# Choosing experts behind the mask and the state's sum: three edits to the VectorE order of a gated recurrence with a cosine router

## The chip, the cores and the metric

The kernel runs on one core of one Trainium2 chip. A core has five engines that run side by side, each through its own queue in order: TensorE (PE in the profile), VectorE (DVE), ScalarE (ACT), GpSimd (POOL) and SyncE (SP), which only starts transfers. The metric is the device time of one execution in microseconds, lower is better; for the kernel before it is the median of five runs.

## The reference

```python
def _attn_ref(q, k, v, alpha):            # (4, 8, 768, 48) each, float32
    state = np.zeros((B, H, D, D))
    for t in range(S):
        state = alpha[:, :, t, :, None] * state + np.einsum('bhd,bhe->bhde', k[:, :, t], v[:, :, t])
        y[:, :, t] = np.einsum('bhd,bhde->bhe', q[:, :, t], state)

def _moe_ref(x, expert_emb, tau, w1, w2): # x: y as (3072, 384) rows; E = 8, F = 1024
    logits = normalized(x) @ normalized(expert_emb).T / tau
    expert_idx = np.argmax(logits, axis=1)
    gate_w = softmax(logits)[np.arange(N), expert_idx]
    for e in range(E):
        mask = expert_idx == e
        h = np.maximum(x[mask] @ w1[e], 0.0)
        out[mask] = gate_w[mask, None] * (h @ w2[e])
```

A gated linear recurrence gives 3072 tokens of 384 numbers; each token goes to the one of eight experts with the largest cosine logit, and the expert's two-layer network, scaled by the softmax weight, is its output.

## The kernel before

The work has two stages. The first does the recurrence in 24 chunks of 128 tokens (NS = 24; six chunks per batch, NCH = 6) and routes the tokens as they come. The second runs the eight experts, one after the other, on the rows sorted by expert. Only the first stage and the turn to the second are touched.

The first stage is a software pipeline. In step s, TensorE in this order turns the alpha, key and query tiles of chunk s (results pa, pk, pq), makes the token rows and logits of chunk s-3 (`rows`, results pyx and px), the scores of chunk s-1 (sc), the output columns of chunk s-2 (`mix_states`, `mix_chunk`), the state's update of chunk s-1 (pd), and turns the decayed keys back (pkb; that belongs to chunk s and is issued at the head of step s+1). The steps can be told apart by the first matmul of pa: 4.70 us is step 0, 81.42 is step 14, 86.33 step 15, 121.88 step 21.

VectorE's regular share of a step is: the scan r (L477), the decayed keys kr (L484), a reciprocal ini (L502), the scan a (L506), the sum of the logits x (L653), the causal mask of one half of the scores, sm (L577), and the state's sum (L558 or L560). A chunk that is the last of its batch has no state update, so no state's sum in the step after. GpSimd multiplies the queries with a (qs, L510), masks the other half of the scores (affine_select, L579), and decays the state (dec, L535; end, L515). ScalarE copies results out of PSUM. The transposes share three PSUM buffers in turn; pd and px share one buffer (tag "mm"), so px of a step can be written only when the state's sum of the step before has read pd.

Routing works on eight groups of chunks:

```python
GROUPS = ((0, 4), (4, 8), (8, 12), (12, 14), (14, 16), (16, 20), (20, 23), (23, 24))
```

Once the rows of a group's last chunk are there, `choose` picks the experts of the group: top (L330), win (L332), win times first (L333), best (L335), chosen (L337), all on VectorE, and then one running sum per chunk, `before` (L340), on GpSimd or, for chunks 15 and 23, on VectorE. This happens at the end of steps 6, 10, 14, 16, 18, 22 and in the two steps after the loop's last chunk. Two or four steps later `place` turns the sums into row numbers with TensorE, and the tokens are scattered to DRAM (`to_rows`, indirect transfers issued by GpSimd), one or two per step.

After chunk 15 is placed, `first_expert` finds which expert is run first (L375 to L389, on VectorE). SyncE needs its result `turn_i` for `fetch_early` (L181), which also waits for the scatters of the first 16 chunks, and for the weights of the first expert (L141). `counts` (L395 to L425) prepares the rest after the last group.

Engines execute in the order in which the program issues, except that a scheduler may move an instruction ahead of others that do not depend on it. `tc.issue_after(x)` keeps what is issued under it behind instruction x on x's own engine; it is an order, not a wait between engines. `behind(s)` is that for the scan a and for qs of step s. Before the change nothing held the choice back, and in the built program it stood between x and sm.

Of the kernel before, what the change touches and what calls it, by code (L numbers as in the profile page):

```python
# [12 lines left out]
ALU = mybir.AluOpType  # L13
# [14 lines left out]
def kernel(  # L28
# [12 lines left out]
    nc = tc.nc  # L41
# [3 lines left out]
    P = 128  # L45
    DP = 64
    NP = H // 2
    NCH = S // P
    N = B * S
    NS = N // P  # L50
# [15 lines left out]
    S0, EARLY = 16, 2  # L66
# [12 lines left out]
    causal = consts.tile([P, 1, P], FP32)  # L79
# [120 lines left out]
    with ExitStack() as c1:  # L200
# [122 lines left out]
        def choose(g):  # L323

            s0, s1 = GROUPS[g]
            n = s1 - s0
            shp = [P, n, E]
            l = x_g[g][:, :, LG : LG + E]
            top = work.tile([P, GMAX], FP32, name="top")[:, 0:n]
            nc.vector.tensor_reduce(top.unsqueeze(2), l, axis=AX.X, op=ALU.max)  # L330
            win = work.tile([P, GMAX, E], FP32, name="win")[:, 0:n]
            nc.vector.tensor_tensor(win, l, bc(top, shp, 2), ALU.is_equal)  # L332
            nc.vector.tensor_tensor(win, win, bc(first, shp, 1), ALU.mult)  # L333
            best = work.tile([P, GMAX], FP32, name="best")[:, 0:n]
            nc.vector.tensor_reduce(best.unsqueeze(2), win, axis=AX.X, op=ALU.max)  # L335
            ch = chosen[:, s0:s1]
            nc.vector.tensor_tensor(ch, win, bc(best, shp, 2), ALU.is_equal)  # L337
            for s in range(s0, s1):
                eng = nc.vector if s in (S0 - 1, NS - 1) else nc.gpsimd
                eng.tensor_tensor(before[:, s + 1], before[:, s], chosen[:, s], ALU.add)  # L340

        def place(g, total=False):
# [29 lines left out]
        def first_expert(n):  # L372

            ok = work.tile([P, E], FP32, name="ok")
            nc.vector.scalar_tensor_tensor(  # L375
                out=ok, in0=n, scalar=float(EARLY * P), in1=first, op0=ALU.is_ge, op1=ALU.mult
            )
            lead = work.tile([P, 1], FP32, name="lead")
            nc.vector.tensor_reduce(lead, ok, axis=AX.X, op=ALU.max)
            nc.vector.tensor_scalar(lead, lead, -1.0, float(E), ALU.mult, ALU.add)  # L380
            nc.vector.tensor_scalar(turn_f, cols, lead, None, ALU.add)
            wrap = work.tile([P, E], FP32, name="wrap")
            nc.vector.tensor_scalar(wrap, turn_f, float(E), float(E), ALU.is_ge, ALU.mult)
            nc.vector.tensor_tensor(turn_f, turn_f, wrap, ALU.subtract)
            nc.vector.tensor_copy(turn_i, turn_f[0:1])
            r0 = work.tile([1, E], FP32, name="r0")
            nc.vector.tensor_scalar(r0, turn_f[0:1], float(N), None, ALU.mult)
            nc.vector.tensor_scalar(r0[:, 0:1], r0[:, 0:1], float(EARLY * P), None, ALU.add)
            nc.vector.tensor_copy(row0, r0)  # L389

        def counts(n):

            shp = [P, E, E]
            mine = work.tile(shp, FP32, name="mine", bufs=1)
            nc.vector.tensor_tensor(  # L395
                mine, bc(turn_f, shp, 2), bc(cols, shp, 1), ALU.is_equal
            )
            nc.vector.tensor_tensor(mine, mine, bc(n, shp, 1), ALU.mult)
            r = work.tile([P, E], FP32, name="rows_of", bufs=1)
            nc.vector.tensor_reduce(r.unsqueeze(2), mine, axis=AX.X, op=ALU.add)  # L400

            row = work.tile([P, E], FP32, name="pad_row", bufs=1)
            nc.vector.tensor_scalar(row, r, part, None, ALU.add)
            end_i = work.tile([P, E], I32, name="end_i", bufs=1)
            nc.vector.tensor_scalar(end_i, r, float(P - 1), None, ALU.add)
            nc.vector.tensor_scalar(end_i, end_i, -P, None, ALU.bitwise_and)
            end = work.tile([P, E], FP32, name="end_f", bufs=1)
            nc.vector.tensor_copy(end, end_i)
            nc.vector.tensor_tensor(end, row, end, ALU.is_ge)
            nc.vector.tensor_scalar(end, end, float(FAR), None, ALU.mult)  # L410
            nc.vector.tensor_tensor(row, row, end, ALU.add)
            nc.vector.scalar_tensor_tensor(
                out=pads, in0=turn_f, scalar=float(N), in1=row, op0=ALU.mult, op1=ALU.add
            )
            nc.vector.tensor_scalar(
                extra, r[0:1], float(HALF - 1 - NC * P), 0.0, ALU.add, ALU.max
            )
            nc.vector.tensor_scalar(extra, extra, 6, None, ALU.arith_shift_right)
            nc.vector.tensor_reduce(most, extra, axis=AX.X, op=ALU.max)
            nc.vector.tensor_scalar(  # L420
                r[:, 0:1], r[:, 0:1], float(-EARLY * P), None, ALU.add
            )
            shp = [P, E, NC + 1]
            nc.vector.tensor_tensor(used, bc(r, shp, 2), bc(starts, shp, 1), ALU.is_gt)
            return nc.vector.tensor_copy(used_i, used[0:1])  # L425
# [31 lines left out]
        def behind(s):  # L457

            queue = ExitStack()
            for call in st[s]["last"]:  # L460
                queue.enter_context(tc.issue_after(call.ins))
            return queue
# [76 lines left out]
        def update(s):  # L539

            c = s % NCH
            if c == NCH - 1:
                return
            d = st[s]
            kb, vt = d["kb"], vt_s[s % NBV]
            pd = ps_mm.tile([P, NP, DP], FP32, tag="mm", name="pd")
            for p in range(NP):
                for hh in range(2):
                    h = 2 * p + hh
                    mm(  # L550
                        pd[DP * hh : DP * hh + DP, p],
                        lhsT=kb[:, h * DP : (h + 1) * DP],
                        rhs=vt[:, h],
                        start=True, stop=True,
                    )
            carried["state"] = state = work.tile([P, NP, DP], FP32, name="state")
            if c == 0:
                nc.vector.tensor_copy(state, pd)  # L558
            else:
                nc.vector.tensor_tensor(state, pd, d["dec"], ALU.add)  # L560

        def scores(s):

            d = st[s]
            kr, qs = d["kr"], d["qs"]
            d["sm"] = sm = [work.tile([P, NP, P], FP32, name=f"sm{hh}") for hh in range(2)]
            sc = [ps_sc.tile([P, NP, P], FP32, name=f"sc{hh}") for hh in range(2)]
            for p in range(NP):
                for i in range(2):
                    to = slice(i * HALF, (i + 1) * HALF)  # L570
                    for hh in range(2):
                        sl = slice(DP * hh, DP * hh + DP)
                        mm(
                            sc[hh][to, p], lhsT=kr[sl, p, to], rhs=qs[sl, p],
                            start=True, stop=True, skip_group_check=True,
                        )
            nc.vector.tensor_tensor(sm[0], sc[0], causal.to_broadcast([P, NP, P]), ALU.mult)  # L577
            nc.scalar.copy(sm[1], sc[1])
            d["masked"] = nc.gpsimd.affine_select(  # L579
                out=sm[1], in_=sm[1], pattern=[[0, NP], [1, P]], base=0,  # L580
                channel_multiplier=-1, compare_op=ALU.is_ge, fill=0.0,
            )
# [115 lines left out]
        def placing(s):  # L698

            n = None  # L700
            for g in placed_at.get(s, ()):
                r = GROUPS[g][1] - 1
                with in_turn():
                    n = place(g, r in (S0 - 1, NS - 1))
                if r == S0 - 1:
                    lead.append(n)
            return n

        lead = []
# [6 lines left out]
        for s in range(NS + 3):  # L716
# [72 lines left out]
            if s >= NS:  # L789
                n = placing(s)  # L790
            if lead:
                with behind(s):
                    first_expert(lead.pop())
            with behind(s) if s < NS else tc.issue_after(st[NS - 1]["masked"].ins):
                n_now = len(send) if s >= NS else 0 if s == NS - 1 else 1 + (len(send) > 2)
                for c in send[:n_now]:
# [8 lines left out]
            for r in rows_of(s):  # L805
                g = group_of[r]
                if r == GROUPS[g][1] - 1:
                    choose(g)
                    with behind(s) if s < NS else ExitStack():
                        nc.gpsimd.tensor_copy(x_g[g][:, :, TK], toks[:, slice(*GROUPS[g])])  # L810
            if s > NS:
                with in_turn():
                    first_layer_early(2 * (s - NS) + 2, 2 * (s - NS) + 4)
        routed = [counts(n)]
        for i in range(2):
            routed.append(to_rows(pads[:, i : i + 1], blank))
            fetch(i)
# [2 lines left out]
    with ExitStack() as c3:  # L820
# [155 lines left out]
        dve = []  # L976
# [408 lines left out]
```

## Time and profile before

| what | value |
|---|---|
| median of 5 runs | 417.6 us (415.79 to 418.26) |
| the profiled execution | 415.63 us, span 413.8 us |
| granted TensorE clock, mean | 0.993 |
| VectorE, GpSimd, ScalarE busy | 69%, 54%, 47% of the span |
| first stage, turn, experts | about 5 to 150, 150 to 168, 168 to 408 us |
| TensorE busy in these | 137.2 of 145, 16.8 of 18, 238.3 of 240 us |

The span runs from the first to the last instruction. The profile counts an engine as busy while it executes; TensorE's matmuls overlap, so its busy share is an upper look at its use. In a timeline line stand the start, the duration, engine, line and operation, what is written and read, and in brackets the idle time before it with what ended it.

### The profile page before, as it was taken

What the parts mean: (1) busy time and instruction counts of PE and PEld (TensorE: products, weight loads), DVE (VectorE), ACT (ScalarE), POOL (GpSimd) and SP (SyncE); (2) the same over time, 40 slices, a digit from 0 to 9 for tenths busy, and PEclk for the clock granted to TensorE, in tenths of its full rate; (3) what the DMA queues carried; (4) which work ended last, traced back from release to release, by engine and by line L of the source; (5) the groups of instructions that cost most, each with busy time, mean ns of one, the idle gap of its engine ahead of it and who ended that gap; (6) DMA issues with size and microseconds to landing.
All of it is one profiled execution on the core that took longest, in us unless ns stands there. A gap on an engine that the chain in (4) does not pass through costs nothing. (4 is left out here: it accounts for less than half of the span.)

```text
span 413.8 us, 12552 instructions
## 1 busy us (share of the span) xinstructions
PE 396.0 (96%) x4954; PEld 353.2 (85%) x4954; DVE 287.2 (69%) x634; ACT 195.4 (47%) x481; POOL 221.7 (54%) x288
## 2 busy tenths in 40 slices
PE   6999999999999999999999999999999999999994
PEld 6889889888888767679989989899979979979974
DVE  7898979699799616862696695791594389397530
ACT  4455544555445524463653734823651572662320
POOL 7455587767765546721853934822761581582001
PEclk9999999999999999999999999999999999999998
DMA  9999999987996993695505606505601900101001
GB/s 139 157 165 157 148 205 180 189 181 164 202 175 131 331 344 134 168 367 197 203 16 171 246 18 224 183 19 184 226 19 41 359 9 19 41 0 41 17 16 44
DMA packets 119379, 60.28 MB, mean 146 GB/s; under 512 B 102287, under 2 KB 113816, under 8 KB 119312
## 3 DMA queue, kind: packets, MB, share of 16 engines
q1 hardware_dynamic: 115208, 49.14, 50.0%
q0 software_dynamic: 3728, 10.16, 6.8%
q8 instruction: 46, 0.75, 0.8%
q14 instruction: 21, 0.17, 0.1%
q10 hardware_dynamic: 376, 0.05, 0.1%
HBM read 49.69 MB, written 11.45 MB: 148 GB/s over the span
## 5 line engine op out<-in xcount | busy, mean ns | idle before, releaser
L852 POOL DMA_INDIRECT out_dram<-y,sx x25 | 24.6, 985 | 102.8 <-DVE y L1161 42.3
L982 DVE TENSOR_TENSOR hT<-pq,hT 128x512 f32<-128x512 f32 x63 | 43.6, 692 | 46.2 <-PE pq L1082 44.3
L1082 PE MATMUL pq<-xT_m,w_m 128*128 128x128 f32 x560 | 67.2, 275 | 0.0
L1082 PEld LDWEIGHTS pq<-xT_m,w_m 128*128 128x128 f32 x560 | 64.7, 192 | 0.3 <-issue 0.3
L510 POOL TENSOR_TENSOR qs<-qc,a 128x512 f32<-128x512 f32 x24 | 30.7, 1277 | 36.7 <-DVE a L506 19.7
L1034 POOL TENSOR_TENSOR w_m<-w_m,w 128x512 f32<-128x512 f32 x30 | 43.2, 1449 | 1.4
L965 PE MATMUL pyo<-w,hT 128*128 128x384 f32 x128 | 42.6, 486 | 0.0
L1082 PE MATMUL pq<-xT_m,w 128*128 128x128 f32 x280 | 38.4, 277 | 0.6
L987 ACT ACTIVATE hT<-hT 128x512 f32<-128x512 f32 x35 | 22.1, 631 | 31.3 <-DVE hT L982 31.3
L1082 PEld LDWEIGHTS pq<-xT_m,w 128*128 128x128 f32 x280 | 34.9, 192 | 2.1 <-issue 1.8
L965 PEld LDWEIGHTS pyo<-w,hT 128*128 128x128 f32 x128 | 23.7, 190 | 14.8
L477 DVE TENSOR_TENSOR_SCAN r<-pa,inr 128x511 f32<-128x511 f32 x24 | 29.2, 1216 | 6.5 <-PE pa L194 4.7
L191 PE MATMUL sc<-qs,kr 64*64 64x128 f32 x768 | 29.5, 272 | 2.6 <-issue 2.6
L311 POOL DMA_INDIRECT xs<-x,dest x24 | 24.2, 1010 | 11.6 <-DVE x L653 6.7
L506 DVE TENSOR_TENSOR_SCAN a<-pa,ini 128x512 f32<-128x512 f32 x24 | 29.3, 1222 | 1.0
L1154 PE MATMUL pq<-w_m,hT_m 128*128 128x192 f32 x168 | 28.4, 326 | 0.0
L1154 PEld LDWEIGHTS pq<-w_m,hT_m 128*128 128x128 f32 x168 | 27.5, 190 | 0.0
L191 PEld LDWEIGHTS sc<-qs,kr 64*64 64x64 f32 x768 | 22.6, 133 | 5.1 <-issue 4.7
L191 PE MATMUL pyx<-sm,vt 128*64 128x128 f32 x384 | 26.3, 279 | 0.0
L649 ACT COPY lg<-pyx 128x32 f32<-128x32 f32 x24 | 4.5, 186 | 44.6 <-PE px L191 38.6
L191 PEld LDWEIGHTS pyx<-sm,vt 128*64 128x64 f32 x384 | 20.5, 136 | 4.1 <-issue 3.4
L1034 POOL TENSOR_TENSOR w_m<-w 128x512 f32<-128x512 f32 x12 | 15.3, 1277 | 15.9 <-PE pq L1082 15.9
(229 smaller groups left out, 914.9 us busy)
## 6 DMA issues: line engine op xcount, KB each, us to landing
w<-in_moe_w_dram SPq DMA_DIRECT2D x16, 1536.0 KB
kt<-in_k_dram SPq DMA_DIRECT2D x24, 192.0 KB
qt<-in_q_dram SPq DMA_DIRECT2D x24, 192.0 KB
vt<-in_v_dram SPq DMA_DIRECT2D x24, 192.0 KB
xg<-xs SPq DMA_DIRECT2D x22, 196.5 KB
at<-in_alpha_dram SPq DMA_DIRECT2D x24, 168.0 KB
xg<-xs SPq DMA_DIRECT2D x8, 98.2 KB
at<-in_alpha_dram SPq DMA_DIRECT2D x24, 22.5 KB
```

The source lines that it names most:

```text
L191: last["pe"] = nc.tensor.matmul(*args, **kwargs)
L311: ins = nc.gpsimd.indirect_dma_start(out=xs, out_offset=bass.IndirectOffsetOnAxis(ap=rows, axis=0), in_=x, in_offset=None, bounds_check=E ...
L477: nc.vector.tensor_tensor_scan(r[:, L - 2 :: -1], pa[:, L - 1 : 0 : -1], inr[:, L - 2 :: -1], 1.0, ALU.mult, ALU.add,)
L506: d["a_scan"] = by_dve = nc.vector.tensor_tensor_scan(a, pa, ini, 0.0, ALU.mult, ALU.add)
L510: by_pool = nc.gpsimd.tensor_tensor(qs.rearrange("p n t -> p (n t)"), d["qc"], a, ALU.mult)
L852: ins = nc.gpsimd.indirect_dma_start(out=out, out_offset=bass.IndirectOffsetOnAxis(ap=col, axis=0), in_=y, in_offset=None, bounds_check=N - 1,
L965: pe[:] = [nc.tensor.matmul(py, lhsT=hT[:, f], rhs=w2_t[:, f], start=(f == 0), stop=(f == FT - 1),)]
L982: dve[:] = [call(*args, **kwargs)]
L987: act[:] = [call(*args, **kwargs)]
L1034: by(to, x, y, op)
L1082: pe[:] = [nc.tensor.matmul(to[:, f], lhsT=left[:, f * P : (f + 1) * P], rhs=right, start=start and f == 0, stop=stop, skip_group_check=Tr ...
L1154: pe[:] = [nc.tensor.matmul(to, lhsT=left[:, f], rhs=right[:, f], start=start and f == 0, stop=stop and f == n - 1, skip_group_check=True,)]
```

## The change

Four edits. The choice of a group is issued behind the last VectorE instruction of the step's mask and state (recorded as "dve"), so it stands behind sm and the state's sum instead of between x and sm. `first_expert` becomes a generator: its first part (up to the first turn_f) is issued behind state and mask of step 20, its second part (turn_i and row0) behind those of step 21. The running sums of a group that holds chunk 15, 22 or 23 are all VectorE's. And `counts` is issued behind the mask of the last chunk.

```diff
             for s in range(s0, s1):
-                eng = nc.vector if s in (S0 - 1, NS - 1) else nc.gpsimd
+                eng = nc.vector if {S0 - 1, NS - 1, NS - 2} & set(range(s0, s1)) else nc.gpsimd
                 eng.tensor_tensor(before[:, s + 1], before[:, s], chosen[:, s], ALU.add)
...
             nc.vector.tensor_scalar(turn_f, cols, lead, None, ALU.add)
+            yield
             wrap = work.tile([P, E], FP32, name="wrap")
...
             nc.vector.tensor_copy(row0, r0)
+            yield
...
             if c == 0:
-                nc.vector.tensor_copy(state, pd)
+                d["dve"] = nc.vector.tensor_copy(state, pd)
             else:
-                nc.vector.tensor_tensor(state, pd, d["dec"], ALU.add)
+                d["dve"] = nc.vector.tensor_tensor(state, pd, d["dec"], ALU.add)
...
-            nc.vector.tensor_tensor(sm[0], sc[0], causal.to_broadcast([P, NP, P]), ALU.mult)
+            d["dve"] = nc.vector.tensor_tensor(sm[0], sc[0], causal.to_broadcast([P, NP, P]), ALU.mult)
...
-                    lead.append(n)
+                    lead.append(first_expert(n))
...
             if lead:
-                with behind(s):
-                    first_expert(lead.pop())
+                with tc.issue_after(st[s - 1]["dve"].ins):
+                    next(lead[0])
+                if s == S0 + 5:
+                    lead.pop()
...
                 if r == GROUPS[g][1] - 1:
-                    choose(g)
+                    with tc.issue_after(st[min(s, NS) - 1]["dve"].ins):
+                        choose(g)
...
-        routed = [counts(n)]
+        with tc.issue_after(st[NS - 1]["dve"].ins):
+            routed = [counts(n)]
```

In the built program GpSimd's sums of a group move too: they wait for `chosen` and stand behind `end` and ahead of `qs` of the next step, where before they stood around affine_select.

## The prediction

> **What bounds the kernel now.** I read the page first: busy times and slices, then its chain of waits. The chain ends in the last scatter to out and reaches back over less than 1% of the span, so it says nothing of the place that changes. The busy line does:
>
> ```profile
> PE 396.0 (96%) x4954; PEld 353.2 (85%) x4954; DVE 287.2 (69%) x634; ACT 195.4 (47%) x481; POOL 221.7 (54%) x288
> ```
>
> TensorE has work nearly always, so the change can gain only what TensorE loses in the 24 steps of the first stage (5 to 150 us); from 168 us on it is busy 238.3 of 240 us and merely starts earlier or later. The listing of waits gives the two that name VectorE's tail and its sum:
>
> ```profile
> PE px L191 <- DVE state L560: 1.2, 1, 1.2
> DVE before L340 <- POOL before L340: 2.0, 1, 2.0
> ```
>
> Where TensorE loses time short of a named wait I took from its timeline: the distance from the first matmul of each part of a step to that of the next. An undisturbed step is 5.3 to 5.4 us (rows 0.51, sc 0.88, back-transpose 0.49). Step 14 and the start of step 15 show the pattern, on VectorE, GpSimd and TensorE in turn:
>
> ```profile
> 84.26 1.22 DVE L506 TENSOR_TENSOR_SCAN a<-pa,ini 128x512 f32<-128x512 f32 x1
> 85.40 0.24 DVE L653 TENSOR_REDUCE x<-lg 128x8 f32<-128x64 f32 x1
> 85.68 0.19 DVE L330 TENSOR_REDUCE top<-x 128x4 f32<-128x32 f32 x1
> 85.90 1.05 DVE L332 TENSOR_TENSOR win<-x,top 128x32 f32<-128x32 f32 x1
> 86.98 0.19 DVE L333 TENSOR_TENSOR win<-win,first 128x32 f32<-128x32 f32 x1
> ...
> 87.57 0.68 DVE L577 TENSOR_TENSOR sm<-sc,causal 128x512 f32<-128x512 f32 x1
> 88.17 0.41 DVE L560 TENSOR_TENSOR state<-pd,dec 128x256 f32<-128x256 f32 x1
> 88.50 1.21 DVE L477 TENSOR_TENSOR_SCAN r<-pa,inr 128x511 f32<-128x511 f32 x1
> ```
>
> ```profile
> 85.63 1.27 POOL L510 TENSOR_TENSOR qs<-qc,a 128x512 f32<-128x512 f32 x1 [1.74 <-ACT ycols L621]
> ```
>
> ```profile
> 88.64 0.26 PE L191 MATMUL px<-sel,ycols 64*64 64x56 f32 x1 [0.56 <-issue]
> ```
>
> The choice stands between x and the mask sm; so state ends only at 88.58, and px, which shares a PSUM bank with the operand of state (tag "mm", one buffer), starts at 88.64, though its first partner pyx was there at 87.76. The profile calls that idle time "issue"; the times tie it to state. Step 21 shows it with lead in place of the choice:
>
> ```profile
> 121.46 0.79 DVE L381 TENSOR_SCALAR turn_f<-cols,lead 128x8 f32<-128x8 f32 x1
> 122.69 0.68 DVE L385 CAST turn_i<-turn_f 1x8 int32<-1x8 f32 x1
> 124.34 0.42 DVE L560 TENSOR_TENSOR state<-pd,dec 128x256 f32<-128x256 f32 x1
> ```
>
> ```profile
> 124.82 0.26 PE L191 MATMUL px<-sel,ycols 64*64 64x56 f32 x1 [1.19 <-DVE state L560]
> ```
>
> **Part 1: the choice behind mask and state.** Five instructions (top to chosen, 85.68 to 87.65: 2.0 us) move behind sm and state in steps 6, 10, 14, 16, 18 and 22. By the instruction order of the two builds, the next r now stands after the third or fourth of them and kr before the last; r and a of the next step are still behind the choice. TensorE's rows part took 0.80 in step 11, 1.29 in step 15, 0.63 in step 17 (counting its late start: state ends at 99.66, rows starts at 99.69) and 0.65 in step 23, against 0.51. That gives 0.29 + 0.78 + 0.12 = 1.19 us, with 0.14 of step 23 counted in part 2. Steps 6 and 18 have no state and give nothing here.
> What is late next? The back-transposes of step s+1 need the PSUM tile that scan a(s+1) reads. In step 15 a ends at 91.85, pkb starts at 92.06. Moved up by 0.78 + 0.29, pkb wants 90.99. VectorE: state needs pd (first matmul 85.27, so about 0.7 us later) and ends at 86.37 on the shifted clock; top, win and win*first at 0.19 each end at 87.05; r, best, kr, chosen, ini and a at their rows' times end at about 90.8. So 0.78 is kept, with 0.2 to spare; if win costs 1.05 again, 0.5 of it goes. win takes 1.05 only because it starts beside qs and ends with it (86.95 against 86.90); in the tail of the stage, with no qs beside it, the same line takes 0.18. I take 0.19, since qs is over by the time win starts in steps 10, 14, 16 and 22.
> The Trainium skill (SBUF — State Buffer, Who interferes with whom) says that a VectorE instruction with two SBUF inputs and a GpSimd instruction that reads SBUF block each other for the whole instruction, the first one winning. The rows above agree; but the rule speaks against the move too, since affine_select (0.64) and dec (0.61) also read SBUF and follow qs. By it win or its product would be held up to 0.6 per choice in the new place, of which the cover in steps 15 and 23 takes little, and the sum below would be near 1.9 instead of 2.7 us.
>
> **Part 2: leading expert in two parts.** In step 20 VectorE spends 120.88 to 123.57 on it (2.7 us with the first of counts), and TensorE's rows in step 21 take 1.92 in place of 0.51: 1.41 lost. Now four instructions follow state(19), six follow state(20), and mine goes behind the mask of step 23 (0.21, no one waits). Part one ends about 1.2 to 1.9 us before today's r(21) start at 124.68, so the 1.41 is won in step 21. But then part two and the choice of step 22 follow in a row. On the clock of before: a(21) ends near 126.5, state(20) near 127.8, part two at 128.7 (each instruction 0.15 to 0.17) or 129.4 (turn_i held beside a scatter as today: 0.68), r(22) after it, a(22) at 132.4 to 133.1, while pkb(22) would want 132.2 and pxe after step 23 wants a(23), which comes at 138.2 to 139.3 against 139.07 now (pxe starts 139.28). So of 1.41 + 0.14, between 0 and 1.1 is left by step 24; I take 0.5, the middle, since one of the two instructions was held in before.
> turn_i comes about 6 us later. Behind it on SyncE stand the early fetch and the first weights; but SyncE waits there until 132.4 for the last token scatter to land (5.0 us in the listing), so some 3 us cover it.
>
> **Part 3: sums on VectorE.** Four of 22 GpSimd sums (0.20 each) become VectorE's (0.17): the first of the two in step 18, and all three of the group that ends with block 22, in the tail. In step 18 VectorE's sum waited 2.04 us for GpSimd's, which was queued behind two scatters (109.59 to 111.88) and affine_select. With it gone, r(19) starts about 2.1 us earlier, and the wait of TensorE in step 19 for scan a (pkb to pa takes 1.04, not 0.49) goes: 0.55. In the tail, GpSimd's three sums (154.27 to 155.06) stood behind four scatters, and place begins at 155.30; on VectorE they end by 151. place is then free once rows(23) is through; that part took 2.22 us, some of it ended by the late second half of ycols, which stays. I take 0.5, bounds 0 and 0.6: everything up to the first fetch (TensorE waits 0.12 for xg at 167.80) follows place.
> GpSimd's remaining sums now stand between end and qs and wait for chosen: 4 take 1.04, while qs waits for a anyway, which comes ini plus scan (1.4 us) after chosen: cover 0.35, and without it qs and the next sc are late by that much.
>
> **Sum.** 1.19 + 0.5 + 0.55 + 0.5 = 2.7 us; by the bounds 1.4 to 3.4. Loads of q, k, v and alpha hold none of it back: TensorE waits for one (qt) for the last time at 42.19, and by their landings in the trace they come over 2.5 us before use from step 10 on. The profiled execution took 415.63 (span 413.8 and 1.8 around it), 2.0 below the median of 417.6: 412.9 on its own footing, 414.9 on the median's, own range 414.2 to 416.2.
>
> **Rivals.** (A) VectorE stays the bound. It is idle only 0.24 us between 117 and 139, so what rows no longer waits for comes back at pkb and pxe; part 2 leaves 0, step 15 loses 0.3, the tail gives nothing: gain about 1.2, 416.4. For it: a(15) clears pkb by 0.2 only. Against: 2.04 of wait and 0.85 for each win leave VectorE. (B) Slower: as win is held by qs today, the moved choice is held by the next GpSimd tensor operations, affine_select and dec (0.64 + 0.61), each time, and a(s+1) with it. Beyond the covers of about 0.2 (step 15), 0.4 (11) and 1.1 (19), that costs 1.05 + 0.85 + 0.15, about 1.2 in step 23 and 1.5 at pkb(22) after the split: 4.75 against 2.7, so 419.6. It decides from a choice of over 2.5 us on. (C) In steps 9, 13, 17 and 19, each after two scatters in a row, the sc part is 1.37, 1.47, 0.66 and 1.15 too long and no row says why. Shifted scatters may lose half of that or add it: 412.6 or 417.2 and more.
>
> **How the numbers follow.** Forecast 0.52, A 0.20, B 0.16, C 0.12. About 0.5% (2.1 us) is what a measurement of this kernel can tell from no change. Of the forecast 0.45 lies beyond it and 0.07 within; A lies within; B has 0.11 beyond on the slow side and 0.05 within; C 0.07 faster and 0.05 slower. Faster 0.52, same 0.32, slower 0.16. The range 412.0 to 419.0 leaves out the far half of B and the ends of C.
>
> **What would show it.** Right: win at about 0.2 in steps 10, 14, 16 and 22; no idle time before px in steps 15 and 21; VectorE's sum in step 18 without a wait; pkb to pa at 0.49 in step 19; place in the tail right after rows. Wrong: win near 0.8 again, idle time before pkb or pa that names scan a in steps 15, 22 and 23, or rows still late with state early.

## The result, and the profile after

| | before | after |
|---|---|---|
| median of the runs | 416.81 us (45 runs) | 414.98 us (24 runs) |
| the profiled execution, its span | 415.63, 413.8 | 413.25, 411.3 |
| granted TensorE clock, mean | 0.993 | 0.992 |

The ratio is 0.9945, 95% interval 0.9928 to 0.9961: faster by 0.55%, 2.3 us. The medians lie only 1.8 us apart; the ratio is not that of the medians, and the longest execution of the kernel after, 418.45, is not in it. The forecast was 414.9, from a gain of 2.7. The size was right and its parts were not: the table sets the terms of the sum against the head start of the changed kernel over the one before, in the two profiled executions (how much earlier TensorE begins each part, read at its first matmul).

| stretch | predicted | measured |
|---|---|---|
| up to step 8 | 0 | 0.62 (a load of q came in time in step 7) |
| steps 8 to 10 | 0 | -0.12 |
| step 11 (choice) | 0.29 | 0.38 |
| step 15 (choice) | 0.78 | 0.56 |
| step 17 (choice) | 0.12 | -0.07 |
| step 19 (sums) | 0.55 | 0.58 |
| step 20 | 0 | 0.18 |
| step 21 (lead) | 1.41 | 1.46 |
| steps 22 and 23 (give-back) | -0.9 | +0.13 |
| last scores, up to the first phe (first layer of the first expert) | 0 | -1.10 |
| tail, up to the last place | 0.5 | -0.06 |

Now the views that answer those of before. The busy line first: VectorE has 2.9 us less to do. TensorE's busy time fell by 0.7 us of the 2.5 us that the span lost, so most of what was won, 1.8 us, was TensorE's idle time.

```profile
PE 395.3 (96%) x4954; PEld 353.1 (86%) x4954; DVE 284.3 (69%) x638; ACT 195.4 (48%) x481; POOL 221.0 (54%) x284
```

VectorE at the turn from step 14 to 15 (timeline of the kernel after; start, duration, engine, line, operation):

```profile
84.53 0.24 DVE L655 TENSOR_REDUCE x<-lg 128x8 f32<-128x64 f32 x1
84.69 0.68 DVE L579 TENSOR_TENSOR sm<-sc,causal 128x512 f32<-128x512 f32 x1
85.29 0.41 DVE L562 TENSOR_TENSOR state<-pd,dec 128x256 f32<-128x256 f32 x1
85.62 0.18 DVE L330 TENSOR_REDUCE top<-x 128x4 f32<-128x32 f32 x1
85.83 0.25 DVE L332 TENSOR_TENSOR win<-x,top 128x32 f32<-128x32 f32 x1
86.11 0.19 DVE L333 TENSOR_TENSOR win<-win,first 128x32 f32<-128x32 f32 x1
86.22 1.21 DVE L479 TENSOR_TENSOR_SCAN r<-pa,inr 128x511 f32<-128x511 f32 x1
```

Mask and state follow x at once: state ends 0.93 us after x (85.70 against 84.77), where it took 2.94. Win takes 0.25 instead of 1.05. In steps 6, 10, 14, 16, 18 and 22 it takes 0.59, 0.19, 0.25, 0.17, 0.58 and 0.24. The long ones are those of steps without a state's sum, where it starts beside qs.

The same at the two halves of the leading expert, steps 20 and 21:

```profile
119.47 0.42 DVE L562 TENSOR_TENSOR state<-pd,dec 128x256 f32<-128x256 f32 x1
...
120.51 0.72 DVE L381 TENSOR_SCALAR turn_f<-cols,lead 128x8 f32<-128x8 f32 x1
121.15 1.21 DVE L479 TENSOR_TENSOR_SCAN r<-pa,inr 128x511 f32<-128x511 f32 x1
...
125.18 0.40 DVE L562 TENSOR_TENSOR state<-pd,dec 128x256 f32<-128x256 f32 x1
125.51 0.43 DVE L384 TENSOR_SCALAR wrap<-turn_f 128x8 f32<-128x8 f32 x1
```

Each half stands behind a state's sum, and TensorE's rows of step 21 take 0.51 instead of 1.92. The sums of the group that ends with chunk 15 follow one another on VectorE, with no wait for GpSimd ahead of the second:

```profile
108.85 0.37 DVE L340 TENSOR_TENSOR before<-before,chosen 128x8 f32<-128x8 f32 x2
```

What is left of TensorE's waits between step 19 and the last place (listing of waits, 103 to 152 us):

```profile
PE sc L191 <- issue: 2.2, 2, 1.9
PE pyx L191 <- ACT ycols L623: 0.5, 2, 0.3
```

Every VectorE name is gone from it. The first line holds what the prediction did not foresee. In the kernel before, TensorE stood idle ahead of the last two matmuls of the last scores like this (TensorE's timeline):

```profile
142.50 0.38 PE L191 MATMUL sc<-qs,kr 64*64 64x128 f32 x2 [0.72 <-issue]
```

and in the kernel after:

```profile
139.89 0.38 PE L191 MATMUL sc<-qs,kr 64*64 64x128 f32 x2 [1.90 <-issue]
```

The head start was 3.74 at the start of these scores and 2.60 behind them.

### The profile page after: what moved, and what is told of

Same layout as the page of the kernel before. It is cut to its first block, busy times and chain, and to the rows that moved or that the text cites. A ratio compares the mean times of both kernels' runs of the same rounds, so it can differ in the third digit from the quotient of the medians.

```text
span 411.3 us, 12556 instructions
## 1 busy us (share of the span) xinstructions
PE 395.3 (96%) x4954; PEld 353.1 (86%) x4954; DVE 284.3 (69%) x638; ACT 195.4 (48%) x481; POOL 221.0 (54%) x284
```

## The experiments

The first theory is that of the prediction: each edit is worth the wait that it takes from TensorE. The twelve runs came in three groups of four, each with its own runs of the kernel before: 410.77, 418.07 and 416.02 us. The first and the third group ran on one chip, the second on another.

### First group: each edit alone, and the lead in one piece

**The choice alone.**

```diff
+                    with tc.issue_after(st[min(s, NS) - 1]["dve"].ins):
-                    choose(g)
+                        choose(g)
```

(with the lines that record "dve")

> The kernel before with the choice alone moved behind mask and state; leading expert, counts and sums stay where they were. Theory 1 (each edit is worth the wait that it takes from TensorE): rows of step 11 go from 0.80 to 0.51, those of step 15 from 1.29 to 0.51, step 17 stays at 0.51 as it did in the kernel after; the start of the pxe transposes moves up by 1.05, the end by 0.9 to 1.2 unless the idle time at the last scores (0.72 in before, 1.90 in after) takes it: 415.7. Rival 1 (what counts is the relief of VectorE as a whole, six wins at 0.2 instead of 1.05): 2 us or more. Rival 2 (the gain of the whole came from a load that was late in step 7, which no edit touches): under 0.3.

Measured: 410.38, ratio 0.9982 (0.9959 to 1.0005). Rows take 0.51 in both step 11 and step 15, as theory 1 has it; in the time the gain stays within the noise, and rival 1 (2 us or more) lies outside the interval, which ends at 1.7. Rival 2 (under 0.3) lies inside it.

This group brought something that was not asked for. The long score parts of steps 9, 13, 17 and 19, which the prediction listed as rival C, are 0.88 in all four kernels of it, and the kernel before took 6.0 us less than in the first comparison (410.77 against 416.81; it has no profile in this group, so that its score parts were short too is inferred from its time). Where they are absent, the wait of VectorE for GpSimd's sum in step 18 costs more (timeline of the choice alone, TensorE):

```profile
109.86 0.66 PE L194 MATMUL pkb<-ident,kr 128*128 128x128 f32 x4 [0.62 <-DVE kr L484]
111.20 0.66 PE L194 MATMUL pa<-ident,at 128*128 128x128 f32 x4 [0.69 <-DVE a L506]
```

With a longer upd part (from the first matmul of pd to that of pkb: 1.25 instead of 0.56) step 19 loses 1.5 us here, where it lost 0.55 before; the score part of the same step, 1.15 too long there, seems to have covered the rest.

**The leading expert alone.**

```diff
-                with behind(s):
-                    first_expert(lead.pop())
+                with tc.issue_after(st[s - 1]["dve"].ins):
+                    next(lead[0])
```

(with the two yields, and the counts behind the last mask)

> The kernel before with only the leading expert in two parts, and the counts behind the last mask; choice and sums stay. Theory 1: rows of step 21 go from 1.92 to 0.51, and nothing of it is given back in steps 22 and 23, so pxe starts 1.4 earlier; the end 1.0 to 1.4 earlier, 415.6, less what the idle time at the last scores takes. Rival (give-back, as the prediction had it: part two and the choice in a row make scan a late): 0.5 or less, with idle time ahead of pkb of step 22 or ahead of pxe that names scan a.

Measured: 410.21, ratio 0.9998 (0.9973 to 1.0023). Rows of step 21 take 0.51, so 1.4 is won; rows of step 23 take 1.57, against 0.65 in the kernel before. VectorE in step 22 shows why:

```profile
128.46 0.24 DVE L655 TENSOR_REDUCE x<-lg 128x8 f32<-128x64 f32 x1
128.74 0.19 DVE L330 TENSOR_REDUCE top<-x 128x4 f32<-128x32 f32 x1
128.96 1.05 DVE L332 TENSOR_TENSOR win<-x,top 128x32 f32<-128x32 f32 x1
...
130.59 0.68 DVE L579 TENSOR_TENSOR sm<-sc,causal 128x512 f32<-128x512 f32 x1
131.20 0.41 DVE L562 TENSOR_TENSOR state<-pd,dec 128x256 f32<-128x256 f32 x1
```

The second half made everything in step 22 late, and the choice, still in its old place, stood ahead of mask and state. So the give-back exists, but it falls on px of step 23 and only where the choice has not been moved: the two edits need each other.

**The sums alone.**

```diff
-                eng = nc.vector if s in (S0 - 1, NS - 1) else nc.gpsimd
+                eng = nc.vector if {S0 - 1, NS - 1, NS - 2} & set(range(s0, s1)) else nc.gpsimd
```

> The kernel before with only the sums of the groups of chunks 14-15 and 20-22 on VectorE. Theory 1: pkb to pa in step 19 goes from 1.04 to 0.49, the tail gives nothing: 0.55, so 416.2. Rival (the tail's term of the prediction holds when the sums alone change): 1.0, with the last place 0.5 earlier after the last rows.

Measured: 408.46, ratio 0.9937 (0.9915 to 0.9960), 2.6 us: more than both expectations. Step 19 has its normal upd and pkb (0.56 and 0.49), 1.5 to 1.9 better than its two neighbours (0.3 of it is lost again in its rows, 0.77), and the last place follows the last rows at once (0.62). In the neighbours it stood behind four scatters and GpSimd's sums; this line is in the waits of the choice alone and of the lead alone:

```profile
PE pyx L191 <- POOL before L340: 1.1, 1, 1.1
```

So the term for the tail was real, 1.1, but not in the runs of the prediction. There the copies of ycols came late, 2.36 us after the first of the matmuls pyx<-sm that they wait for (147.96), against 0.70 in the sums alone (145.85). Scatters stand beside them in both, so this goes with the long score parts and is open like them. ScalarE's timeline of the kernel after:

```profile
150.32 0.37 ACT L623 COPY ycols<-pyx 128x256 f32<-128x256 f32 x1 [2.46 <-PE pyx L191]
```

and of the sums alone:

```profile
146.55 0.81 ACT L621 COPY ycols<-pyx 128x256 f32<-128x256 f32 x2 [0.81 <-PE pyx L191]
```

**The lead in one piece.**

```diff
-            yield          # the one behind the first turn_f
...
-                if s == S0 + 5:
-                    lead.pop()
+                lead.pop()
```

> The kernel after, but the leading expert in one piece, behind the mask and state of chunk 19 in step 20. Theory 1 (split matters): some 2 to 2.5 us of VectorE work in one step make the next scans r and a late; TensorE idles 0.6 to 1.4 in steps 21 and 22 (ahead of pkb or pa), and the time is that much above after's: about 415.6 to 416.0 where before is at 416.8. Rival (the place behind the state is all, the split nothing): no idle time named after a scan in steps 21 and 22, and the time of after within 0.3, about 414.6.

Measured: 406.72 (6 runs), ratio 0.9893 (0.9857 to 0.9929). No idle time in steps 21 and 22 names a scan; the rival looks right, but this group had no run of the kernel after to compare with. With all edits the gain is 4.4 us here (4.1 by the medians), not 2.3: 1.07 of the choice, 1.5 of the lead, 1.7 of step 19 and 1.1 of the tail make 5.4, and the part from the last scores to phe took back 0.5 to 1.2 (3.50 against 2.3 to 3.0 in its neighbours).

### Second group: the weights behind the last scores

**Before and after once more.**

> The kernel before once more, for a profile beside the next runs. The four kernels of the first set of runs had no long score parts in steps 9, 13, 17 and 19 (0.88 each), and the kernel before was 410.8 there, 6.0 under its 416.8 elsewhere. Theory C1 (these stretches, together 4.6 us, belong to the occasion and not to the order of instructions): before runs at 410 to 411 when its score parts take 0.88 in these steps, and at 415 to 418 when they take 1.5 to 2.4. Theory C2 (the edits took them away): before has them at any time.

> The kernel after once more, against before on one chip. If the score parts are short in both, step 19 of before loses 1.5 to 1.9 to the wait for the sum (that is what it lost with choice or lead alone changed: parts upd and pkb 1.25 to 1.55 and 1.34 instead of 0.56 and 0.49) and the last place waits 1.1 for GpSimd's sum. Theory 1 then gives 1.05 + 1.46 + 1.7 + 1.1 less some 1 at the first weights: 4 us, near 406.7. Rival (the gain of the first comparison, 2.3, is the same everywhere): 408.5.

Measured: before 419.81 in the profiled run, 418.07 its median; after 416.53, ratio 0.9972 (0.9943 to 1.0002). The score parts of steps 9, 13, 17 and 19 are long again in both (2.36, 2.41, 1.58, 2.01 in before; 2.04, 2.34, 1.51, 2.10 in after), at the same lengths as in the first two profiles. C1 holds as far as the profiles go: the parts belong to the occasion, and the edits did not take them away.

**w1 ahead of the early fetch.**

```diff
                     if c == S0 - 1:
+                        weights(0, (1,))     # w1 alone
                         fetch_early()
...
-                    weights(0)
+                    weights(0, (2,))         # w2
```

(`weights` is given the parts that it loads)

> The kernel after, with the load of the first expert's w1 issued ahead of the early fetch of its rows, so that it needs only turn_i and not the last scatter; w2 stays where it was. Theory W (after the last scores TensorE stands still, 1.90 us in after, since the instructions that follow arrive late behind the transfers of w1 and w2, and then waits for w1): w1 lands about 3 us earlier, so the wait for w1 is gone; the idle time of the code stays unless its fetch now falls clear of the transfers; 0.4 to 2 us faster than after. Rival (idle time belongs to the last scores themselves, a scatter or an engine): same place, same length, no gain.

Measured: 416.56, ratio 0.9948 (0.9917 to 0.9979); not told apart from after. The w1 transfer was issued 3.0 us earlier (127.31 instead of 130.29 in the first profile of after), and TensorE's idle time came earlier and a second time:

```profile
135.12 0.54 PE L193 MATMUL sc<-qs,kr 64*64 64x128 f32 x9 [1.47 <-issue]
...
141.40 0.38 PE L193 MATMUL sc<-qs,kr 64*64 64x128 f32 x2 [1.41 <-issue]
```

It follows the transfers, not the last scores. The trace's transfer records name what it waits for. TensorE's instructions arrive as 16 KB transfers on a queue of their own ("q8 instruction" on the page); between the starts of two of them lie about 255 TensorE instructions on average in the first stage. While w1 and w2 move, one is late: in the kernel after 440 instructions lie between two, in the one before 333. Each time the idle time ends shortly after that transfer's end (in the seven profiles not shown the distance is 1.30 to 1.49):

| profile | transfer ends | matmuls go on | distance |
|---|---|---|---|
| before | 141.10 | 142.50 | 1.40 |
| after | 138.43 | 139.89 | 1.46 |
| choice alone | 136.02 | 137.42 | 1.40 |
| lead alone | 137.06 | 138.31 | 1.25 |
| sums alone | 135.80 | 137.26 | 1.46 |
| lead in one piece | 133.83 | 135.14 | 1.31 |
| w1 first, both times | 133.81, 140.03 | 135.12, 141.40 | 1.31, 1.37 |

The place says the same. Counted over all of TensorE's instructions in the trace, the idle time stands ahead of the same one, number 5826, in thirteen profiles; with w1 first, in both kernels that have it, there is one ahead of number 5571. The two places are 255 instructions apart, about what one transfer brings.

Nothing in TensorE's queue waits there: the two matmuls carry no wait, and the wait for w1 stands behind them. In after it costs nothing more; in the lead alone and the sums alone phe waited another 0.41 and 0.48 for w1.

**The lead in one piece, w1 first.**

> The kernel after with the leading expert in one piece behind the mask and state of chunk 19, and w1 issued ahead of the early fetch. With turn_i some 5 us earlier than in after, w1 is issued as soon as the last loads of v are out, and lands over 3 us ahead of its use. Theory W: no wait for w1 at phe; 1 to 2.4 us below the whole piece alone (406.7 where before was 410.8), so 404.5 to 406 there. Rival (in one piece costs more than the split, as the first theory had it): 0.4 to 1.4 above the same with the split, e5.

Measured: 417.35, ratio 0.9989 (0.9957 to 1.0021): no gain. The last scores take 0.99 without idle time; it has moved to step 23 (0.88 at 135.06). The early rows are late:

```profile
139.92 0.85 PE L196 MATMUL pxe<-ident,xg 128*128 128x128 f32 x6 [2.29 <-DMA xg<-xs]
```

The last token scatter was issued at 126.8 and w1 at 127.1; the scatter landed at 135.10, behind w1, where with the split it landed at 129.90. SyncE issued the early fetch only then. What TensorE gained at the last scores it lost at pxe, the transposes of these rows.

### Third group: split or not, w2, and single scatters

**After once more, and w2 a step later.**

```diff
-                    weights(0)
+                    weights(0, (1,))
...
+                weights(0, (2,))
                 weights(1)
```

> The kernel after once more, as the measure for the three that are built on it. Where the score parts of steps 9, 13, 17 and 19 take 1.5 to 2.4, it should stand 1 to 2.3 under before; where they take 0.88, about 4 under it, as the sum of what choice, lead and sums alone showed there.

> The kernel after, with the load of the first expert's w2 taken out from behind that of w1 and issued a step later, ahead of the second expert's weights; its first use is some 20 us after that. Theory W (TensorE stands still at the last scores because a 16 KB fetch of its instructions comes late while 3 MB of weights are moved: in ten profiles the idle time ended 1.25 to 1.46 after the end of that fetch): the fetch falls at the end of or after w1's 5 us, the idle time goes from 1.3 to 1.9 to 0.3 or less, w1 lands earlier, and the time is 1.0 to 1.9 below after's. Rival (it is the wait for w1 or the scores themselves): w1 lands no earlier than it is issued plus 8, phe starts when it did, no gain.

Measured: after 414.33, ratio 0.9955 (0.9927 to 0.9983), which repeats the first result. With w2 later 414.36, ratio 0.9953 (0.9928 to 0.9978). The edit didn't do what it says: SyncE has nothing to wait for between the two loads, so w2 was issued at 131.28, 0.9 us behind w1, against 0.6 in after. It is one more run of after and says nothing on theory W; a w2 that is truly late was not tried.

**The lead in one piece, on the same.**

> As the run before (w2 a step later), and the leading expert in one piece behind the mask and state of chunk 19. Against that run it tells what the split is worth. Theory 1 (the split spares scan a in steps 20 to 22): 0.4 to 1.4 slower than with the split. Rival (the place behind the state is what counts): the same within 0.3, with pkb and pa of steps 21 and 22 free of idle time, as the run of the whole piece showed in all but 0.38 us of step 22.

Measured: 414.18, ratio 0.9946 (0.9915 to 0.9977), 0.2 below the run with the split. The times alone can't exclude the 0.4 of theory 1, but the traces do: the head start of this run over the one with the split is 0.22 in step 19 and 0.15 at the last scores, so in between the split won less than 0.1. The reason is in VectorE's timeline of this run: in one piece, too, the next scan goes ahead of the second half.

```profile
120.56 0.72 DVE L383 TENSOR_SCALAR turn_f<-cols,lead 128x8 f32<-128x8 f32 x1
121.19 1.21 DVE L480 TENSOR_TENSOR_SCAN r<-pa,inr 128x511 f32<-128x511 f32 x1
122.32 0.25 DVE L385 TENSOR_SCALAR wrap<-turn_f 128x8 f32<-128x8 f32 x1
```

Being behind the state is what counts.

**One scatter a step in steps 8 and 12.**

```diff
-                n_now = len(send) if s >= NS else 0 if s == NS - 1 else 1 + (len(send) > 2)
+                n_now = len(send) if s >= NS else 0 if s == NS - 1 else 1 + (s >= S0 and len(send) > 2)
```

> The kernel after with one scatter a step, not two, in steps 8 and 12; the two in a row in steps 16 and 18 stay. Theory C3 (the long score part of a step comes of two scatters in a row in the step before): score parts of steps 9 and 13 go from 2.0 to 2.4 to 0.88, those of steps 17 and 19 stay at 1.5 to 2.1; 2.5 to 3.0 below after's time, and nothing else moves, since these scatters are waited for only at the early fetch. Rival (they come of the placing of a group, whatever the number of scatters): score parts of 9 and 13 stay long. Where the chip shows no long score parts at all, the time is after's.

Measured: 412.53 (6 runs), ratio 0.9889 (0.9847 to 0.9930), 1.8 us below after by the medians of one group; the intervals just touch. Score parts of steps 9 and 13 take 0.90 and 0.88, those of 17 and 19 stay at 1.48 and 2.03: C3 holds. TensorE in step 9, with two scatters in the step before (the run with w2 later):

```profile
53.70 0.67 PE L193 MATMUL sc<-qs,kr 64*64 64x128 f32 x15
54.64 0.44 PE L193 MATMUL sc<-qs,kr 64*64 64x128 f32 x4 [0.28 <-issue]
55.35 0.69 PE L193 MATMUL sc<-qs,kr 64*64 64x128 f32 x13 [0.28 <-issue]
```

and with one:

```profile
53.31 1.12 PE L191 MATMUL sc<-qs,kr 64*64 64x128 f32 x32
```

Of the 2.7 us won there only 0.9 is left by step 16 (against after in the same group), since the queries of steps 13 to 15 now arrive late:

```profile
85.48 0.63 PE L194 MATMUL pq<-ident,qt 128*128 128x128 f32 x4 [0.75 <-issue]
```

The profile says "issue"; TensorE's queue waits there for the semaphore of the load of qt (the landing of its last piece is not in the trace), and the other wait there, for ScalarE's copy of kb, had ended at 84.49. The cover of 2.5 us that the prediction gave these loads was gone in this run. Shorter steps alone don't explain it: in the first group, with score parts as short, three of the four profiles show no such wait in steps 13 to 15. Its median is the lowest found where the long parts appear.

## Why the prediction was right, and where it was not

**Part 1 held in mechanism and price.** State no longer waits for the choice, and win in its new place costs 0.19, 0.25, 0.17 and 0.24 where 0.19 was taken. The rule that spoke against it (the Trainium skill, SBUF — State Buffer, Who interferes with whom) was there in one of these four places: in step 22 win times first ran from 131.24 for 0.68 beside affine_select, which started at the same 131.24 and took 0.64. That is 0.5 once, not up to 0.6 per choice, and VectorE had the time. The term was mis-sized by 0.3: in step 15 scores took 1.11 instead of 0.88, and step 17 gave nothing.

**Part 2: the 1.41 came (1.46), the give-back did not.** The failing step is "a(22) at 132.4 to 133.1, while pkb(22) would want 132.2". On the same clock a of step 22 ended at 131.84 (129.73 in after, and the head start of 2.11 at the start of step 21). The prediction had r of step 22 behind all six instructions of part two; it went ahead of the last two. And turn_i took 0.16, not 0.68; of the others only wrap was held (0.43 instead of 0.17). The head start went from 3.57 to 3.70 over steps 22 and 23. The lead alone showed that the fear was sound for another order. In the sum the 1.0 too little here was made up by 1.1 that was lost at a place the prediction never looked at, the instruction transfers beside w1 and w2.

**Part 3: step 19 as said (0.58 for 0.55), the tail not.** The 0.5 was made to hang on place, with "the late second half of ycols, which stays" named but not weighed; it was the bound, so nothing came. In the first group it was not, and the same edit gave 1.1.

**Loads.** "Loads of q, k, v and alpha hold none of it back" held. But 0.57 of the measured head start is one load that was late in step 7 of the profile of before and not in that of after. It belongs to no edit (in the third group's profile of after that part of step 7 took 0.88, against 0.98 in before and 0.44 undisturbed), and without it the profiled gain is 1.9.

**Rivals.** A (VectorE stays the bound) and B (held by affine_select) fell: no VectorE name is left in TensorE's waits. C was the right place to be uneasy, though not as a risk of the change: the long parts stayed the same.

So the number was right partly by luck. In the profiled pair 1.0 (give-back), 0.6 (load) and 0.2 (step 20) too little stand against 1.1 (last scores), 0.6 (tail) and 0.3 (choice) too much. And the forecast set out from 417.6, the median of five runs, where 45 runs gave 416.81: 414.9 was met with a gain of 1.8 by the medians, not 2.7.

## What to carry to other kernels

A gain in a queue is worth what the next wait leaves of it, and that wait depends on the occasion: the same sums were worth 0.5 us by the profiles of the first comparison (step 19 and the tail) and 2.6 by the times of the first group. Before trusting a sum of small terms, look at every stretch that no row explains, and follow the path a few steps beyond the last edit to the next place where transfers pile up. And edits to one queue are to be costed together: the lead alone gave nothing that can be measured, because the choice in its old place stood in the way.

## What the runs showed of the hardware

Two scatters in a row can stop TensorE for 0.6 to 1.5 us in the step after, in short pauses that no wait explains, and ScalarE's copies of its results come late with it (in step 9 the copy of the logits started at 55.47 after two scatters, at 53.70 after one, with the scores begun at 53.70 and 53.31); one scatter does not. In one group of runs two in a row did it neither. What differs between the groups stays open; it is not the chip alone, since that group and the third, with long parts, ran on one chip.

A 16 KB transfer of TensorE's own instructions, late beside 3 MB of weights, stopped it for 0.6 to 2.1 us. That it is the cause is inferred from the nearly constant distance of 1.25 to 1.49 us in fourteen profiles, from the two places 255 instructions apart, and from the idle time moving with the transfers; taking the weights away was not tried.

Idle time can cost twice. In the run with single scatters the first six matmuls of phe took 2.40 instead of 1.46 to 1.49 right after an idle time, and the windows view (length, busy times of the engines, PEclk, DMA share, GB/s) shows a lower granted clock:

```profile
137.00:150.00 13.00, 11.14 (x122) 8.19 (x122) 2.71 (x13) 3.20 (x10) 2.70 (x5) 0.87 1.01 365
```

against a stretch around the same place in after, third group (it begins 4.4 us ahead of the first phe, the one above 2.2):

```profile
135.00:148.00 13.00, 12.28 (x214) 9.67 (x210) 4.64 (x18) 5.54 (x18) 5.22 (x9) 1.00 0.98 366
```

A mean of 0.87 over 13 us is half speed for 3.4 us (0.13 times 13, doubled), 1.7 us of TensorE's time. Seven of the fourteen profiles have such a spell between 139 and 162 us, always at the end of idle time or right after it, either this one or the one ahead of the last place; others with as much idle time have none. It explains part of why the runs of after spread over 411.8 to 418.5, but not all: with a granted clock of 0.996 or more they took 411.8 to 415.2, under 0.990 they took 414.1 to 416.7, and in between anything from 412.3 to 418.5. The Trainium skill (TensorE: Matmul & The Clock Gate, Part 1) describes a free-running activity window of 3.4 us and half speed after an idle one; the length agrees with these rows, but here TensorE was still busy for 39% to 72% of the 3.4 us ahead of such a spell.
